# Layer 1 of a four-layer kernel begins on x and C alone, with TensorE on zeros until they come

## The chip, the cores and the metric

The kernel runs on one core of a Trainium2 chip. The metric is the device time of one execution in microseconds, lower is better. Before the change the median of three runs is 1193.91 us (1193.26 to 1196.67).

## The reference, cut to what matters

Four layers follow one another on x of 2048 x 576 (fp32): Fourier mixing, H3 convolution, Fourier mixing, H3 convolution. Each adds its result to x.

```python
def _A_ref(x, dft_seq_re, dft_seq_im, dft_hid_re, dft_hid_im):
    a = jnp.einsum("bsd,ed->bse", x, dft_hid_re)
    b = jnp.einsum("bsd,ed->bse", x, dft_hid_im)
    return jnp.einsum("ts,bse->bte", dft_seq_re, a) - jnp.einsum("ts,bse->bte", dft_seq_im, b)
...
x = x + _A_ref(_layernorm(x, axis=-1), ...)        # layer 1
x = x + _B_ref(_layernorm(x, axis=-1), B_k, B_v, B_shift_k, B_ssm_k, B_ssm_D)
x = x + _A_ref(_layernorm(x, axis=-1), ...)
x = x + _B_ref(_layernorm(x, axis=-1), B_k, B_v, B_shift_k, B_ssm_k, B_ssm_D)
```

`_B_ref` shifts k by a causal convolution of 4 taps, multiplies it with v, convolves that over the sequence with `ssm_k` by FFT, adds `ssm_D` times it, and multiplies with the normalised x. The FFT part doesn't depend on x, so one result serves both H3 layers.

## The kernel before, in words

**Layer 1** (`layer`, called with `get_x0`) multiplies the sequence DFT matrix C with the normalised x before the hidden DFT. Its work is cut into steps `(g, tb, k)`: for each of 4 blocks `tb` of 512 output columns, for the real and the imaginary matrix `g`, over 16 row blocks `k` of 128 rows. A step has 14 matmuls of 128x512: 12 into the four banks `s` (4 column groups of x, each high times high, high times low, low times high) and 2 into `rm`, which holds the remaining 64 columns. Every operand is split in a high part (rounded to fp32r by ScalarE) and a low part (the difference, by VectorE).

**A row of x** is loaded by SP (`load_x`), and gets its layer norm in pieces. `stats0` starts it: for rows 0 to 7 (`normed`, `norm_stats`) VectorE takes the statistics (lines 181 to 183) and GpSimd a power for the reciprocal root (line 184); then VectorE makes the bias (line 190) and ScalarE scales (line 191). From row `ASTAT` = 8 on (`normed_x`, `sums`) ScalarE sums (lines 649, 651), with GpSimd's power in line 653. `to_x` rounds (line 195) and makes the two low pieces (lines 197, 198). `get_x0(j)` does this for row j and starts the statistics of row j + 1; a step asks for the rows up to `XLEAD` = 3 ahead.

**A tile of C** is loaded by `load_c` into one of a few raw slots and split by `split` (lines 98 and 99) into one of three slots.

**The H3 stage** (`branch`, advanced by `next(br)`) fills VectorE, ScalarE and the gaps in TensorE's order meanwhile: it loads v, ssm_k, k and constants (`f1_loads`), splits rows (`f1_split`, lines 98 and 99), convolves k (lines 393 to 398), and multiplies with constants (`f1_products`, matmuls into the banks `bf`, which ScalarE evacuates in line 451). The main loop advances it to a wanted count at each half step, `want`, from `used` on. Six pieces are taken before the loop starts; with them come the first two H3 products, ahead of layer 1's first matmul.

**The order of the work** on each engine is a list scheduler's, which takes instructions by program order as they become ready in its own timing. `tc.issue_after(i)`, and `behind(...)` which nests several, queue what a block traces on the engine of `i` behind `i`; they order one engine's instructions and wait for no end. The lists `biased`, `rounded`, `made`, `halved`, `parted`, `stored`, `scaled` and `anchor` hold the instructions that serve as such marks: bias of a row, its rounding, its low half, the split of a C tile, that of an H3 row, an evacuation, a scaling, the load of a C tile. All loads of C, x and H3 rows share SP's queue; the H3 constants go through GpSimd's queue (`load_fr`), or through SP and a conversion on ScalarE when no power has been asked for yet.

Of the kernel before, what the change touches and what calls it, by code (L numbers as in the profile page):

```python
# [10 lines left out]
F32 = mybir.dt.float32  # L11
FR = mybir.dt.float32r
AF = mybir.ActivationFunctionType
OP = mybir.AluOpType

P = 128
# [3 lines left out]
J = S // P  # L20
TB = 4
NT = 512
# [3 lines left out]
EPS = 1e-5  # L26
ASTAT = 8
# [3 lines left out]
K_FIRST = 4  # L31
F1_16 = 5
VW = 384
F1_END = 42
W_FROM = 41
HOLD = 125
# [29 lines left out]
def fnet_h3_kernel(ctx: ExitStack, tc: tile.TileContext, x, c_mat, w_re, w_im, k_pad, v, shift_k,  # L66
                   ssm_k, ssm_d, f1c, i2c, midc, out):
    nc = tc.nc
# [5 lines left out]
    def mm(ps, lhsT, rhs, first, last, more=False):  # L74
        return nc.tensor.matmul(ps, lhsT, rhs, start=first, stop=last, skip_group_check=more).ins  # L75
# [3 lines left out]
    def turn():  # L79
        given[0] += 1  # L80
        return banks[(given[0] - 1) % 3]
# [15 lines left out]
    def split(h, l, src):  # L97
        a = nc.scalar.activation(h, src, AF.Copy).ins  # L98
        return a, nc.vector.tensor_tensor(l, src, h.bitcast(F32), OP.subtract).ins  # L99

    @contextmanager
    def behind(*instructions):
        with ExitStack() as stack:
            for i in instructions:
                stack.enter_context(tc.issue_after(i))
            yield
# [11 lines left out]
    def region_b(dt, name):  # L118
        return sb.tile([P, 6 * WIDE], dt, tag="rb", name=name)
# [9 lines left out]
    ring = {}  # L129

    def lay(t, at, *sizes):

        for name, words, n in sizes:
            ring.setdefault(name, Ring()).tiles.extend(t[:, at + i * words:at + (i + 1) * words] for i in range(n))
            at += n * words
        assert at <= t.shape[1], (at, t.shape, sizes)
        return at

    def fresh(*names):
        for name in names:  # L140
            ring[name] = Ring()
# [5 lines left out]
    xs = mats[:, :X_END].rearrange("p (j n) -> p j n", j=J)  # L147
# [13 lines left out]

    anchor, made, rounded, pows, biased, halved, added, evac, parted, stored = [], [], [], [], [], [], [], [], [], []

    scaled = []

    def load_after(dst, src):
        with tc.issue_after(anchor[-1]):
            return nc.sync.dma_start(dst, src).ins
# [8 lines left out]
    def norm_stats(src):  # L177
        m = ring["stat"]()
        st, mv, ve, rs = m[:, :12].rearrange("p (a c) -> p a c", a=2), m[:, 12:14], m[:, 14:15], m[:, 15:16]
        for i in range(2):  # L180
            nc.vector.bn_stats(st[:, i, :], src[:, i * HD:(i + 1) * HD])
        nc.vector.bn_aggr(mv, st)
        nc.vector.tensor_scalar(ve, mv[:, 1:2], EPS, None, op0=OP.add)  # L183
        pows.append(nc.gpsimd.tensor_tensor(rs, ve, mhalf, OP.pow).ins)  # L184
        return mv, rs, m[:, 16:17]

    def normed(src, y):
        mv, rs, nb = norm_stats(src)
        yield
        biased.append(nc.vector.tensor_scalar(nb, mv[:, 0:1], rs, -1.0, op0=OP.mult, op1=OP.mult).ins)  # L190
        scaled.append(nc.scalar.activation(y, src, AF.Identity, bias=nb, scale=rs).ins)

    def to_x(y, j):
        t = xs[:, j, :]
        rounded.append(nc.scalar.activation(t[:, :D], y, AF.Copy).ins)
        h = t.bitcast(F32)
        nc.vector.tensor_tensor(t[:, D:D + REM], y[:, NC * P:], h[:, NC * P:D], OP.subtract)
        made.append(nc.vector.tensor_tensor(t[:, D + REM:], y[:, :NC * P], h[:, :NC * P], OP.subtract).ins)
        return t
# [10 lines left out]
    X = [None] * J  # L210
    CT = {}

    def load_c(step):
        g, tb, k = step
        raw = ring["craw"]()
        anchor.append(load_after(raw, c_mat[g, tb, k]) if anchor else nc.sync.dma_start(raw, c_mat[g, tb, k]).ins)
        c = ring["cs"]()
        t = c[:, :NT], c[:, NT:]
        with behind(*stored):
            halved[:] = split(t[0], t[1], raw)  # L220
        CT[step] = t

# [77 lines left out]
    def layer(get_x, xres, done, pending, blocks=TB):  # L300
        steps = [(g, tb, k) for tb in range(blocks) for g in range(2) for k in range(J)]
        for n, (g, tb, k) in enumerate(steps):
# [3 lines left out]
            if n + 2 < len(steps):  # L306
                load_c(steps[n + 2])
# [41 lines left out]
    def branch():  # L349
# [3 lines left out]
        at = lay(flts, SC_AT + CRAW * NT, ("so", D, 4), ("land", D, 3))  # L353
        lay(flts, SC_AT + CRAW * NT, ("sp", 2 * VW, 3))
        lay(flts, at, ("craw", NT, 1))
# [103 lines left out]
        for n, (j, src) in enumerate(todo):  # L459
# [6 lines left out]
            elif src:  # L466
                visits += [(2 * n + 3, j, fcs[j], xf, at, VW, "sp", at) for at in range(0, 2 * D, VW)]
            if n:
# [203 lines left out]
    def normed_x(src, y, junk):  # L672
        sm, rs, nb = sums(src, junk)
        yield
        nc.vector.tensor_tensor(nb, sm, rs, OP.mult)
        nc.scalar.activation(y, src, AF.Identity, bias=nb, scale=rs)

    XL, LN = {}, {}

    def load_x(j):  # L680
        if j < J:
            XL[j] = ring["x"]()
            nc.sync.dma_start(XL[j], x[:, j, :])

    def stats0(j):
        if j < J and j not in LN:
            src = XL.pop(j)
            LN[j] = src, normed_x(src, src, ring["junk"]()) if j >= ASTAT else normed(src, src)
            next(LN[j][1])

    def get_x0(j):
        if X[j] is None:
            if j > 0:
                load_x(j + 2)
            stats0(j)
            if j > 0:
                with behind(*stored):
                    stats0(j + 1)
            src, ln = LN[j]
            with behind(*rounded[-1:]):  # L700
                next(ln, 0)
            X[j] = to_x(src, j)
# [32 lines left out]
    def done1(j, xa):  # L735
# [7 lines left out]
        if j < J - 1:  # L743
            nc.sync.dma_start(out[:, j, :], q)

    pending = []
    lay(flts, SC_AT, ("craw", NT, CRAW))
    br = branch()
    wl = load_w()
    load_x(0)  # L750
    next(br)
    get_x0(0)
    with tc.issue_after(biased[0]):
        next(br)
        with behind(*parted, scaled[0]):
            load_c((0, 0, 0))
        load_x(1)
        with behind(rounded[0]):
            load_c((0, 0, 1))
        load_x(2)  # L760
    used = 4
    first_lo = parted[1]
    next(br)
    next(br)
    with behind(first_lo):
        get_x0(1)
    next(br)
    next(br)
    spent = passed = 0.0
    total = (I2_END + 1 - MID_FROM) * STEP + 3 * 2 * TB * PIECE  # L770
    work = 64 * 3.1 + 32 * I2_COST
    for n, whole in layer(get_x0, lambda j: x[:, j, :], done0, pending):
        part = whole == "part"
        if part:
            whole = False
        if (whole or whole is not None and n % J < J - 1) and n <= F1_END and not part:
            at = n if whole else n - 0.5
            at16 = 4 + 2 * F1_16
            want = int(4 + F1_16 * at / 8 if at <= 16 else at16 + (68 - at16) * (at - 16) / (F1_END - 16))
            with behind(made[min(n + 2, J - 1)], *evac):  # L780
                while used < want:
                    next(br)
                    used += 1
        if whole is not None and not part and n >= W_FROM and len(W) < 9:
            with behind(*stored):
                next(wl)
        if whole and n == MID_LOAD:
            next(br)
        if n >= MID_FROM:
            if whole is not None:  # L790
                share = (5 if whole else 3) if n % J < J - 1 else (8 if whole else 6)
                passed += STEP * share / 14 * BORDER.get(n % J, 1.05)
            if whole is None or whole and n % 2 == 1 and n % (2 * J) < J - 1 and pending:
                finish(pending, 1)
                passed += PIECE
            while spent < work * min(1.0, passed / total):
                with behind(*added, *evac):
                    spent += next(br, work)
        if not whole:
            continue  # L800
        if n >= W_SAVE and n % 2 == 0:
            next(wl, 0)
        m = n - PREP
        if m == 0:
            lay(flts, SC_AT + CRAW * NT + 2 * D, ("xa", D, 2), ("yb", D, 2))
            old = ring["craw"]
            held = [old(), old()]
            fresh("craw")
            lay(flts, SC_AT + CRAW * NT + 6 * D, ("craw", NT, 1))
            ring["craw"].tiles.extend(held)  # L810
            gate = region_b(F32, "gate")
            lay(gate, 0, ("xa", D, 4), ("yb", D, 4), ("xj", D, 2))
        if 0 <= m and n < HOLD:
            advance(m // 2 if m % 2 == 0 and m < 2 * EARLY else None)
# [127 lines left out]
    cs, done = {}, []  # L942
# [67 lines left out]
    loaded, builds = [], []  # L1010
    for n, whole in layer(get_x1, lambda j: xb_d[j], done1, pending, 1):
# [12 lines left out]
        if n == STATIC:  # L1024
            t7.append(region_a(FR, "t7"))
            at = lay(flts, SC_AT + CRAW * NT, ("csum", WIDE, 3), ("rems", 2 * REM, 2))
# [27 lines left out]
    for ch in range(9):  # L1054
        first = ch + 2 if ch < 4 else ch + 6 if ch < 8 else 18
# [103 lines left out]
```

## Time and profile before

| | before |
|---|---|
| median of three runs | 1193.91 us |
| the profiled execution, its time | 1195.03 us |
| its span in the profile | 1193.3 us |
| TensorE busy | 1172.4 us, 98% of the span |
| VectorE busy | 840.3 us, 70% |
| ScalarE busy | 661.1 us, 55% |
| GpSimd busy | 75.6 us, 6% |
| mean granted TensorE clock | 0.998 |

A row of a timeline gives the start, the time that the piece took, the engine, the line and operation, what it writes from what it reads, its shape and number, and in brackets the idle time before it with what ended it. PE is TensorE, DVE VectorE, ACT ScalarE, POOL GpSimd; a q behind the name is the queue that issues DMAs. `s`, `rm` and `bf` are TensorE's banks, `mats` holds the split x and C, `flts` the fp32 work space, `early` the rows of x, `f1r` and `f1f` the H3 stage's tiles. A row of the waits names who waited, for whom, how long in all, how often and the longest.

### The profile page before, as it was taken

To read this page: it belongs to the slowest core of one execution; us is meant where nothing else is said; L and a number is where in the kernel's file an instruction comes from. 1 tells how busy PE (TensorE), PEld (TensorE's weight loads), DVE (VectorE), ACT (ScalarE), POOL (GpSimd) and SP (SyncE) were. 2 spreads that over 40 slices of the span, in tenths; PEclk is the share of its full clock that TensorE was granted. 3 is DMA by queue.
4 is the path that set the end of the run, shared out by engine and by line. 5 is a ranking of instruction groups with operands and counts; after the bars stand their busy time and mean duration, and the time that the engine had idled before them with its cause. 6 is when DMAs were issued, how large, how long until landed. Compare 5 with 4: busy or idle time off the path is not lost.

```text
span 1193.3 us, 18055 instructions
## 1 busy us (share of the span) xinstructions
PE 1172.4 (98%) x6248; PEld 996.3 (83%) x6248; DVE 840.3 (70%) x1498; ACT 661.1 (55%) x1311; POOL 75.6 (6%) x116
## 2 busy tenths in 40 slices
PE   7999999999999999999999999999999999999997
PEld 5776667888888888888988898888888888889997
DVE  7899983679777677685347756865776777774764
ACT  7865655679877668775435666634444445450210
POOL 2210000000000000001101121000000000001111
PEclk9999999999999999999999999999999999999999
DMA  9869898546666656648957676872672777895621
GB/s 327 306 199 311 263 295 269 167 133 188 217 194 211 206 174 203 207 133 272 295 193 236 230 246 226 267 260 71 220 277 76 220 278 258 248 334 158 217 86 41
DMA packets 142846, 259.85 MB, mean 218 GB/s; under 512 B 15649, under 2 KB 43553, under 8 KB 142754
## 3 DMA queue, kind: packets, MB, share of 16 engines
q1 hardware_dynamic: 102674, 205.45, 53.1%
q10 hardware_dynamic: 33168, 42.63, 10.3%
q0 software_dynamic: 6912, 10.62, 3.5%
q8 instruction: 49, 0.80, 0.3%
q14 instruction: 43, 0.35, 0.1%
HBM read 191.99 MB, written 66.65 MB: 217 GB/s over the span
## 4 chain that ended last, share of the span: by engine, by line
PE 76%; ACT 3%; DVE 1%; issue 1%; DMA 0%; POOLq 0%; ACTq 0%; DVEq 0%; SPq 0%
PE s L75 43%; PE bk L75 30%; PE rm L75 4%; ACT flts L512 1%; ACT mid L512 1%; ACT u L98 0%; DMA wd<-w 0%; ACT mats L98 0%; DVE mid L518 0%; DVE flts L534 0%; DVE flts L533 0%; DVE flts L531 0%; DVE flts L532 0%; DVE mats L99 0%; POOLq L1155 0%
## 5 line engine op out<-in xcount | busy, mean ns | idle before, releaser
L75 PE MATMUL s<-mats 128*128 128x512 f32 x2088 | 540.9, 395 | 2.4 <-DVE mats L99 0.8
L75 PEld LDWEIGHTS s<-mats 128*128 128x128 f32 x2088 | 380.9, 188 | 84.8 <-issue 10.4
L99 DVE TENSOR_TENSOR mats<-flts,mats 128x512 fp32r<-128x512 f32 x206 | 141.1, 689 | 63.8 <-ACT mats L98 62.5
L98 ACT ACTIVATE mats<-flts 128x512 fp32r<-128x512 f32 x206 | 128.5, 629 | 82.0 <-PE bk L75 35.0
L75 PE MATMUL bk<-mid 128*128 128x288 f32 x768 | 131.9, 298 | 2.4 <-ACT flts L512 1.6
L75 PEld LDWEIGHTS bk<-mid 128*128 128x128 f32 x768 | 116.9, 188 | 20.0 <-ACT flts L512 6.3
L75 PE MATMUL bk<-w,u 128*128 128x288 f32 x864 | 121.0, 296 | 0.4 <-DVE w L241 0.4
L75 PEld LDWEIGHTS bk<-w,u 128*128 128x128 f32 x864 | 117.5, 188 | 4.0 <-ACT flts L512 1.2
L518 DVE TENSOR_TENSOR mid<-flts,mid 128x576 fp32r<-128x576 f32 (+1 forms) x149 | 93.5, 628 | 34.9 <-ACT mid L512 30.9
L512 ACT ACTIVATE flts<-bk 128x288 f32<-128x288 f32 x160 | 62.1, 404 | 86.8 <-PE bk L75 77.7
L75 PE MATMUL rm<-mats 128*128 128x512 f32 x304 | 94.8, 391 | 0.0
L512 ACT ACTIVATE flts<-flts 64x288 f32<-64x288 f32 x192 | 85.0, 443 | 5.5
L512 ACT ACTIVATE mid<-flts 128x576 fp32r<-128x576 f32 (+1 forms) x148 | 80.4, 575 | 7.6 <-DMA flts<-td 3.2
L451 ACT ACTIVATE flts<-bf 128x384 f32<-128x384 f32 (+1 forms) x104 | 43.2, 463 | 45.6 <-PE bf L75 45.5
L287 DVE TENSOR_TENSOR flts<-flts,bk 128x288 f32<-128x288 f32 x48 | 21.8, 454 | 65.9 <-PE bk L75 65.8
L75 PE MATMUL bk<-mats 128*128 128x288 f32 (+1 forms) x376 | 67.8, 317 | 0.0
L75 PEld LDWEIGHTS rm<-mats 128*128 128x128 f32 x304 | 56.9, 188 | 12.3 <-DVE flts L273 0.2
L75 PE MATMUL s<-t,mats 128*128 128x512 f32 x264 | 64.9, 389 | 0.0
L184 POOL TENSOR_TENSOR flts<-flts 128x1 f32<-128x1 f32 x35 | 29.2, 834 | 522.0 <-DVE flts L183 520.0
L75 PE MATMUL bk<-mats,t 128*128 128x288 f32 (+1 forms) x368 | 59.3, 303 | 0.0
L75 PEld LDWEIGHTS bk<-mats 128*128 128x128 f32 x376 | 55.5, 188 | 3.4
L75 PEld LDWEIGHTS s<-t,mats 128*128 128x128 f32 x264 | 49.5, 188 | 10.3
(145 smaller groups left out, 1467.5 us busy)
## 6 DMA issues: line engine op xcount, KB each, us to landing
flts<-in_c_mat SPq DMA_DIRECT2D x148, 256.0 KB, 3.6
ph<-in_c_mat SPq DMA_DIRECT2D x54, 512.0 KB, 4.5
flts<-in_c_mat SPq DMA_DIRECT2D x30, 512.0 KB, 5.0
flts<-td SPq DMA_DIRECT2D x53, 288.0 KB, 3.0
td<-flts ACTq DMA_DIRECT2D x36, 384.0 KB, 4.5
vd<-flts ACTq DMA_DIRECT2D x64, 144.0 KB, 2.5
flts<-vd SPq DMA_DIRECT2D x32, 288.0 KB, 4.6
mid<-in_i2c POOLq DMA_DIRECT2D x32, 256.0 KB, 4.9
```

Source lines behind the costliest of these rows:

```text
L75: return nc.tensor.matmul(ps, lhsT, rhs, start=first, stop=last, skip_group_check=more).ins
L98: a = nc.scalar.activation(h, src, AF.Copy).ins
L99: return a, nc.vector.tensor_tensor(l, src, h.bitcast(F32), OP.subtract).ins
L184: pows.append(nc.gpsimd.tensor_tensor(rs, ve, mhalf, OP.pow).ins)
L287: added[:] = [nc.vector.tensor_tensor(r[:, cs], r[:, cs], ps[:, :HD], OP.add).ins]
L451: stored[:] = [nc.scalar.activation(so[:, i, :], ps[i], AF.Copy).ins]
L512: last_act.append(nc.scalar.activation(*args, **kw).ins)
L518: nc.vector.tensor_tensor(l, src, h.bitcast(F32), OP.subtract)
```

## The change

- SP's first loads become x row 0, C tile 0, x row 1, C tile 1, x row 2. The H3 stage's first loads follow behind row 2, and its first constant goes through GpSimd behind the power of row 1.
- `warm` clears 512 columns of the slot of row 15 on VectorE, and TensorE multiplies it with itself 18 times into a `bf` bank.
- The first C tile's high half is made ahead of row 0's scaling, its low half on VectorE behind the statistics of row 1. The rows 1 and 2 are started by hand, in a fixed order, ahead of the loop.
- Before the loop one piece of the H3 stage is taken instead of six; the wanted count is held to `2 * at - 2` in the first steps. The pieces queue behind later marks: the rounding of the row after, and up to step 7 the newest loads of x and C.
- In the loop, a row's statistics on VectorE queue behind the low half two rows before, for rows up to 7; the C split of the first 16 steps queues behind the rounding of row k - 2; x loads queue behind the newest C load. Rows from 8 on, whose statistics are ScalarE's, get no such mark.

```diff
+WARM = 18
...
-    scaled = []
+    scaled, varied = [], []
...
-        nc.vector.tensor_scalar(ve, mv[:, 1:2], EPS, None, op0=OP.add)
+        varied.append(nc.vector.tensor_scalar(ve, mv[:, 1:2], EPS, None, op0=OP.add).ins)
...
-    def load_c(step):
+    def raw_step(step):
         g, tb, k = step
         raw = ring["craw"]()
         anchor.append(load_after(raw, c_mat[g, tb, k]) if anchor else nc.sync.dma_start(raw, c_mat[g, tb, k]).ins)
+        return raw
+
+    def load_c(step, raw=None):
+        raw = raw_step(step) if raw is None else raw
         c = ring["cs"]()
         t = c[:, :NT], c[:, NT:]
-        with behind(*stored):
+        with behind(*stored, *rounded[step[2] - 2:max(0, step[2] - 1) if step[:2] == (0, 0) else 0]):
             halved[:] = split(t[0], t[1], raw)
...
-            nc.sync.dma_start(XL[j], x[:, j, :])
+            loaded.append(nc.sync.dma_start(XL[j], x[:, j, :]).ins)
...
             if j > 0:
-                load_x(j + 2)
+                with behind(anchor[-1]):
+                    load_x(j + 2)
             stats0(j)
             if j > 0:
-                with behind(*stored):
+                with behind(*stored, *made[j - 1:j if j < ASTAT - 1 else 0]):
                     stats0(j + 1)
...
+    def warm():
+        t = xs[:, J - 1, :NT]
+        nc.vector.memset(t.bitcast(F32), 0.0)
+        b = turn()
+        for i in range(WARM):
+            mm(b, t[:, :P], t, i == 0, i == WARM - 1)
...
     load_x(0)
-    next(br)
-    get_x0(0)
-    with tc.issue_after(biased[0]):
+    raws = []
+    for i in range(2):
+        with behind(loaded[-1]):
+            raws.append(raw_step((0, 0, i)))
+        with behind(anchor[-1]):
+            load_x(i + 1)
+    warm()
+    stats0(0)
+    first = ring["cs"]()
+    CT[0, 0, 0] = first[:, :NT], first[:, NT:]
+    nc.scalar.activation(first[:, :NT], raws[0], AF.Copy)
+    next(LN[0][1], 0)
+    with behind(biased[0]):
+        stats0(1)
+    with behind(loaded[-1]):
         next(br)
-        with behind(*parted, scaled[0]):
-            load_c((0, 0, 0))
-        load_x(1)
-        with behind(rounded[0]):
-            load_c((0, 0, 1))
-        load_x(2)
-    used = 4
-    first_lo = parted[1]
-    next(br)
-    next(br)
-    with behind(first_lo):
-        get_x0(1)
-    next(br)
-    next(br)
+    with behind(varied[1]):
+        low = nc.vector.tensor_tensor(first[:, NT:], raws[0], first[:, :NT].bitcast(F32), OP.subtract).ins
+        X[0] = to_x(LN[0][0], 0)
+    with behind(made[0]):
+        next(LN[1][1], 0)
+    with behind(biased[1], rounded[0]):
+        load_c((0, 0, 1), raws[1])
+    with behind(halved[1]):
+        stats0(2)
+    used = -1
...
-            want = int(4 + F1_16 * at / 8 if at <= 16 else at16 + (68 - at16) * (at - 16) / (F1_END - 16))
-            with behind(made[min(n + 2, J - 1)], *evac):
+            want = int(min(2 * at - 2, 4 + F1_16 * at / 8) if at <= 16 else at16 + (68 - at16) * (at - 16) / (F1_END - 16))
+            with behind(made[min(n + 2, J - 1)], *evac, *rounded[min(n, 4) + 1:min(n, 4) + 2],
+                        *(loaded[-1:] + anchor[-1:] if n < 8 else [])):
```

More of the change, by code (lines that the diff above doesn't have):

```diff
@@ L676, in normed_x @@
         nc.scalar.activation(y, src, AF.Identity, bias=nb, scale=rs)
[L678 removed]
+    XL, LN, loaded = {}, {}, []
     def load_x(j):
```

## The prediction

> **What bounds the kernel now.** I read the page first, then the waits of TensorE, then the timelines of TensorE and of all engines over the first 60 us, since the diff touches nothing that runs later than layer 1's first blocks.
>
> ```profile
> span 1193.3 us, 18055 instructions
> PE 1172.4 (98%) x6248; PEld 996.3 (83%) x6248; DVE 840.3 (70%) x1498; ACT 661.1 (55%) x1311; POOL 75.6 (6%) x116
> ```
>
> TensorE is busy for 1172.4 of 1193.3 us, so 20.9 us is all the idle time there is. The waits say where much of it lies:
>
> ```profile
> PE bf L75 <- DVE f1r L99: 6.7, 1, 6.7
> PE bf L75 <- ACT flts L451: 1.2, 2, 1.1
> PE s L75 <- DVE mats L99: 0.8, 1, 0.8
> PE s L75 <- ACT mats L195: 0.8, 1, 0.8
> ```
>
> The first 6.7 us are the wait for the first operand; the fourth line is one stall inside block 0 (at 55.6 us, below). What this leaves out is how fast TensorE runs once it has started. Its timeline:
>
> ```profile
> 6.71 1.09 PE L75 MATMUL bf<-f1r 64*128 64x288 f32 x6 [6.71 <-DVE f1r L99]
> 7.94 0.79 PE L75 MATMUL s<-mats 128*128 128x512 f32 x1
> 9.58 0.79 PE L75 MATMUL s<-mats 128*128 128x512 f32 x1 [0.84 <-DVE mats L99]
> 10.40 1.09 PE L75 MATMUL bf<-f1r 64*128 64x288 f32 x6
> 11.42 3.86 PE L75 MATMUL s<-mats 128*128 128x512 f32 x10
> 15.12 0.62 PE L75 MATMUL rm<-mats 128*128 128x512 f32 x2
> 15.57 2.90 PE L75 MATMUL s<-mats 128*128 128x512 f32 x12
> 18.31 0.62 PE L75 MATMUL rm<-mats 128*128 128x512 f32 x2
> 18.77 2.88 PE L75 MATMUL s<-mats 128*128 128x512 f32 x12
> 22.03 0.67 PE L75 MATMUL bf<-f1r 64*128 64x288 f32 x6
> 22.63 3.05 PE L75 MATMUL s<-mats 128*128 128x512 f32 x12
> 27.42 0.66 PE L75 MATMUL bf<-f1r 64*128 64x288 f32 x6
> 29.95 2.88 PE L75 MATMUL s<-mats 128*128 128x512 f32 x12
> ```
>
> Twelve matmuls of 128x512 run from 15.57 to 18.31, 0.228 us each; the ten from 11.42 to 15.12 took 0.370 each. An H3 product (six bf matmuls) is 1.09 us twice at the beginning and 0.66 later. So TensorE runs slow until it has been dense for some time. If a slow matmul takes twice a fast one (the products bound the ratio below, at 1.65), 6.2 of the ten were slow, and the fast rate came at 11.42 + 6.2 x 0.456 = 14.25, that is 3.85 us after the dense run began at 10.40.
>
> From 15.57 on TensorE has no gap up to 55 us. A step (12 s and 2 rm matmuls) is 18.77 - 15.57 = 3.20. A product adds 22.63 - 22.03 = 0.60, or up to 0.78 with its gaps when it stands inside a step; I take 0.70. By 29.95 five steps and four products are done: 5 x 3.20 + 4 x 0.70 = 18.8 us of work. **Lost up to there: 29.95 - 18.8 = 11.15 us.** This is the quantity the change works on.
>
> **The change part by part.** The chain that brings the first matmul of layer 1, and the loads beside it, now:
>
> ```profile
> 0.74 0.39 SPq L683 DMA_DIRECT2D early<-in_x  x1
> 0.81 0.06 DVE L174 MEMSET flts<- 128x1 f32 x1 [0.81 <-PEq L1151]
> 1.18 0.42 SPq L418 DMA_DIRECT2D flts<-in_ssm_k  x1
> 3.76 0.82 DVE L181 BATCH_NORM_STATS2 flts<-early 128x6 f32<-128x288 f32 x2 [2.89 <-DMA early<-in_x]
> 4.48 0.68 ACT L98 ACTIVATE f1r<-flts 128x576 fp32r<-128x576 f32 x1 [2.24 <-DMA flts<-in_ssm_k]
> 4.62 0.21 DVE L182 BATCH_NORM_AGGREGATE flts<-flts 128x2 f32<-128x12 f32 x1
> 4.86 0.15 DVE L183 TENSOR_SCALAR flts<-flts 128x1 f32<-128x1 f32 x1
> 5.10 0.55 POOL L184 TENSOR_TENSOR flts<-flts 128x1 f32<-128x1 f32 x1 [4.65 <-DVE flts L183]
> 5.68 0.21 DVE L190 TENSOR_SCALAR flts<-flts 128x1 f32<-128x1 f32 x1 [0.67 <-POOL flts L184]
> 5.93 0.87 ACT L191 ACTIVATE early<-early,flts 128x576 f32<-128x576 f32 x1
> 7.23 0.67 ACT L195 ACTIVATE mats<-early 128x576 fp32r<-128x576 f32 x1
> 7.75 1.18 DVE L181 BATCH_NORM_STATS2 flts<-early 128x6 f32<-128x288 f32 x3 [1.19 <-DMA early<-in_x]
> 8.85 0.68 DVE L99 TENSOR_TENSOR mats<-flts,mats 128x512 fp32r<-128x512 f32 x1
> 9.44 0.22 DVE L197 TENSOR_TENSOR mats<-early,mats 128x64 fp32r<-128x64 f32 x1
> 9.57 0.68 DVE L198 TENSOR_TENSOR mats<-early,mats 128x512 fp32r<-128x512 f32 x1
> ```
>
> *x and C alone.* x row 0 stays the first load, so its statistics still begin at 3.76 and its bias still ends at 5.89. The C tile moves to the second place on SP; what is second today (288 KB) landed at 4.48, so C's high half (0.61 on ScalarE) is made by 5.1, ahead of the scaling. The scaling stays at 5.93. Rounding no longer stands behind a C split: 5.93 + 0.89 + 0.67 = 7.5 instead of 7.90. The first operand pair is ready at 7.5.
>
> *The low halves.* Row 1 of x, in the fifth place today, was waited for until 7.75; in the third it has 832 KB up to its end (288 + 256 + 288) against 1248 (288 + 288 + 128 + 256 + 288). Between row 0 at 3.7 and 7.75, in proportion to the bytes, that is 6.05 (bounds 5.5 and 6.6). The new order sends VectorE through row 1's statistics before C's low half: 6.05 + 0.86 + 0.24 + 0.1, so C low at 7.25 to 7.92 and x low, by the spacings of 8.85, 9.44 and 9.57, at 7.97 to 8.65. Today they end at 9.53 and 10.25. A low-half product that must wait until 8.7 delays a column by at most 8.7 - 7.5 - 0.46 = 0.75; high products of the other three columns, 0.9 us and more of them, can stand in between if the scheduler puts them there. Cost between 0 and 0.75; I take 0.1, since the high halves are ready sooner in any timing.
>
> *Row 1 in time for step 1.* GpSimd's power for row 1 falls among VectorE's three two-input operations. Rows that show what this does:
>
> ```profile
> 11.27 0.73 DVE L429 TENSOR_TENSOR flts<-flts,f1f 1x576 f32<-1x576 f32 x1
> 11.45 0.99 POOL L184 TENSOR_TENSOR flts<-flts 128x1 f32<-128x1 f32 x1 [5.16 <-DVE flts L183]
> 49.10 2.62 DVE L393 TENSOR_TENSOR f1f<-f1f 128x1152 f32<-128x1152 f32 x2
> 49.27 4.13 POOL L653 TENSOR_TENSOR flts<-flts 128x1 f32<-128x1 f32 x1 [7.69 <-DVE flts L652]
> ```
>
> A power is 0.55 alone, 0.99 when it was issued inside a two-input operation of VectorE (it ended 0.44 after it), and 4.13 when such operations followed one another. So row 1's ends at 8.65 + 0.44 = 9.1, its bias at 9.3, scaling and rounding at 10.9, its low half near 11.75. Step 0, dense from 7.6, ends at 10.8: a wait of 0.1 to 0.3, I take 0.2. Rows 2 and 3 follow at 2.4 to 2.8 us each by the same spacings, below the 3.20 of a step, so the lead grows.
>
> The Trainium skill (SBUF — State Buffer, "Who interferes with whom") says that a VectorE instruction with two SBUF inputs contends with a GpSimd instruction that reads SBUF, and the later one blocks fully; the two pairs of rows above agree (0.99 and 4.13 against 0.55). By it the change, which puts such operations beside row 1's power, could lose what it wins; what that gives here is the case of the held powers, below.
>
> *Zeros.* A memset of 128x512 on VectorE is not in the trace; it lies between the 0.06 of the 128x1 memset and the 0.68 of a two-input 128x512 operation, ends between 0.9 and 1.6, and hides under the wait for x until 3.76. TensorE begins near 1.5. Slow for 3.85 us, that is 8.4 matmuls at 0.456; the other 9.6 at 0.228 take 2.2: the zeros end at 7.55, just when x is ready. If the slow time is 4.9 (10.40 to 15.3, the latest the rows allow) they end at 8.05; all slow, at 9.7. They cost between 0 and 0.55 (2.2 if they never bring the fast rate, the third case) and I take 0.05.
>
> The Trainium skill (TensorE: Matmul & The Clock Gate, Part 1) says that the array runs at half clock until a free-running window of about 3.4 us has been busy. The 3.85 above fits; by this rule the zeros would end between 7.2 and 8.8, and the sum would come out the same or up to 1.2 us later.
>
> *The H3 stage.* Its first loads move behind x row 2 on SP, its constants to the GpSimd queue behind row 1's power, its two first products from before step 0 into step 3. By the wanted counts both versions have taken eight pieces by the end of step 4 (before 6 + 2, after 1 + 7), so the same four products are done there, at the fast rate. Two products in each of steps 3 and 4 ask ScalarE for about 0.7 + 0.7 more a step than now; the lead of the rows pays for it, as this rounding of row 8 shows, done while TensorE is still at row 5 (the step that begins at 29.95):
>
> ```profile
> 31.81 0.69 ACT L195 ACTIVATE mats<-early 128x576 fp32r<-128x576 f32 x1
> ```
>
> New SP orders (x and H3 loads behind the newest C load) put loads behind C loads that wait for a raw slot; that slot is free one step before. I take 0 for both; if a lead is gone the price is the third case.
>
> **Sum.** Lost after the change: 7.5 (first operands) + 0.05 (zeros) + 0.1 (low halves) + 0.2 (row 1) = 7.85. Gain 11.15 - 7.85 = **3.3 us**, bounds 2.1 (0.75, 0.55 and 0.3 all paid) and 3.65 (all dense from 7.5). Behind step 4 the order of work is as before and TensorE-bound, so the shift holds to the end. The profiled execution: span 1193.3 becomes 1190.0, with 1.7 us around it (1195.0) 1191.7; the median of the runs, 1193.9, stands 1.1 under the profiled run, so 1190.6.
>
> **The rivals.**
>
> *Block 0's stall goes too.*
>
> ```profile
> 55.65 0.67 ACT L195 ACTIVATE mats<-early 128x576 fp32r<-128x576 f32 x1
> ```
>
> TensorE waited 0.8 us for this rounding of row 12, whose power is the one that took 4.13. In another phase of VectorE's convolution the power takes 0.55 and the stall vanishes: gain 3.3 + 0.8 = 4.1, 1189.8. For it: the early pieces are reshuffled. Against it: behind step 4 the same orders stand.
>
> *The start is eaten.* Either the zeros don't bring the fast rate (9.7 at the end of the zeros, then 3.85 us at half rate cost another 1.9: lost 11.6, 1194.4), or row 12, which has no slack, doesn't come 3.3 us sooner, because its chain hangs on VectorE and GpSimd and not on TensorE, and the stall grows to 4.1: 1193.9. Against the second: ScalarE waits on TensorE too (its evacuations and ring slots), so its pace follows.
>
> *Slower: held powers.* Rows 9 to 15 get their powers from GpSimd while VectorE runs the convolution's two-input operations. Each power held as at 49.27 delays its row by 4.13 - 0.55 = 3.6. It decides as soon as the row's slack is under 3.6, which 3.3 us less lead brings about. Two more held rows: 2 x 3.6 - 3.3 = 3.9 slower, 1197.8. Against it: one such row in seven now.
>
> *It doesn't do what it says:* matmuls on zeros queued late or x not first would show a first real matmul near 7.9 and no gain; it is part of the third case.
>
> **How the numbers follow.** Forecast 0.50, stall gone 0.26, eaten 0.10, slower 0.14. A measurement of this kernel tells about 0.3%, 3.6 us, from no change; the forecast's own range, 1189.6 to 1191.8 (its bounds, and the 0.65 by which the fastest run shown lies under the median), has four tenths of its chance beyond that bound. Faster 0.26 + 0.20 = 0.46, same 0.30 + 0.10 = 0.40, slower 0.14. The range leaves out the slower case and takes in the rest: from 1188.8 (3.65 and 0.8 gained, 0.65 of scatter) to 1194.6 (eaten, with 0.7).
>
> **What would show it.** Right: zeros from about 1.5 to 7.6; first s matmul on x between 7.5 and 8; ten s matmuls of step 0 at 0.228; the fifth step ending near 26.7 instead of 29.95; TensorE's busy time up by the zeros, about 6 us. Wrong in a step: row 0's statistics later than 3.8 (loads), s matmuls at 0.37 after 8 (zeros don't count), a wait on mats L195 or L198 in steps 1 to 4 (rows late), a wait on flts L451 in steps 3 and 4 (evacuations). Wrong altogether: a fifth step at 27 and the end not earlier, which would put the loss into rows 9 to 15 or behind them.

## The result: 0.9% slower, and the profile after

After the change the median of five runs is 1207.05 us (1204.66 to 1207.64), beside 1194.33 for the kernel before in the same session: ratio 1.0091, 95% interval 1.0072 to 1.0111 (the ratios here and below are not quotients of the medians shown). The forecast was 1190.6, its range ended at 1194.6. The profiled execution took 1207.05, its span is 1205.3, 12.0 more than before.

The page of the kernel after, then its waits of TensorE:

```profile
span 1205.3 us, 18096 instructions
PE 1180.1 (98%) x6266; PEld 1000.5 (83%) x6266; DVE 840.7 (70%) x1499; ACT 659.8 (55%) x1310; POOL 76.8 (6%) x117
```

```profile
PE bf L76 <- DMA f1r<-in_f1c: 6.0, 1, 6.0
PE bk L76 <- ACT flts L517: 4.0, 10, 1.3
PE bk L76 <- DVE flts L292: 1.5, 2, 0.8
PE bf L76 <- DVE mats L754: 1.5, 1, 1.5
```

TensorE's share is 98% as before: it is busy 7.7 us longer, of which the 18 zeros are 6.5. The wait of 6.7 us for the first operand became one of 1.5 (for the memset of the zeros). Two others are new or larger: one of 6.0 us appeared, on a DMA that brings an H3 constant, and `bk`, the accumulators of layer 2's stage, far from the diff, waited 1.6 and 0.7 us for evacuations before and 4.0 and 1.5 after. The timeline of TensorE shows the start and the wait for the constant:

```profile
1.49 6.70 PE L76 MATMUL bf<-mats 128*128 128x512 f32 x18 [1.49 <-DVE mats L754]
8.03 3.24 PE L76 MATMUL s<-mats 128*128 128x512 f32 x12
11.57 2.88 PE L76 MATMUL s<-mats 128*128 128x512 f32 x12
22.72 3.02 PE L76 MATMUL s<-mats 128*128 128x512 f32 x12
32.24 1.09 PE L76 MATMUL bf<-f1r 64*128 64x288 f32 x6 [6.05 <-DMA f1r<-in_f1c]
33.26 4.83 PE L76 MATMUL s<-mats 128*128 128x512 f32 x12
37.93 0.61 PE L76 MATMUL rm<-mats 128*128 128x512 f32 x2
```

Up to 26.2 us it looks as forecast, with steps 0 to 4 dense and from step 1 on at the fast rate, but two H3 products are done by then and not the four forecast. Then nothing for 6.05 us, and the work behind it is slow again: a product of 1.09 and a step's 12 matmuls in 4.67 (33.26 to 37.93) instead of 2.74. The windows of the same stretch, whose columns are the stretch, its length, the busy time and number of instructions of each engine, the granted clock of TensorE, the DMA share and GB/s:

```profile
26.20:32.20 6.00, 0.00 (x0) 0.00 (x0) 2.62 (x6) 2.42 (x6) 0.70 (x2) 0.85 1.07 372
32.24:33.26 1.02, 1.02 (x7) 0.74 (x7) 0.00 (x0) 0.00 (x0) 0.00 (x0) 0.50 1.13 382
33.26:37.23 3.97, 3.97 (x11) 3.13 (x10) 1.99 (x5) 3.62 (x8) 0.56 (x1) 0.51 0.90 348
37.23:41.00 3.77, 3.77 (x21) 2.79 (x19) 1.83 (x4) 1.80 (x5) 0.00 (x0) 1.00 0.09 35
```

The clock falls in the wait (0.85 as a mean), stays at 0.5 for the next 5.0 us and is full from 37.2 on. So the constant costs 6.05 + 0.43 (product) + 1.93 (step) = 8.4 us. Why it was late stands in GpSimd's timeline and in the DMA view of 20 to 34 us:

```profile
8.72 0.69 POOL L173 DMA_DIRECT2D f1r<-in_f1c  x1
23.53 0.55 POOL L185 TENSOR_TENSOR flts<-flts 128x1 f32<-128x1 f32 x1 [3.32 <-DVE flts L184]
24.03 0.58 POOL L173 DMA_DIRECT2D f1r<-in_f1c  x1
```

```profile
f1f<-in_k_pad SPq DMA_DIRECT2D x3, 576.0 KB, 8.7
f1f<-in_shift_k SPq DMA_DIRECT2D x2, 576.0 KB, 9.8
f1r<-in_f1c POOLq DMA_DIRECT2D x3, 128.0 KB, 8.3
```

One constant serves two products. The first is asked for behind row 1's power, at 8.72. The second, which the third product needs at 26.2, is asked for only behind row 6's power, at 24.03, and takes some 8 us to land, among 2.9 MB that SP has just asked for. Before, it was asked for behind row 0's power, far ahead of the third product, which ran at 22.03:

```profile
5.10 0.55 POOL L184 TENSOR_TENSOR flts<-flts 128x1 f32<-128x1 f32 x1 [4.65 <-DVE flts L183]
5.60 0.69 POOL L172 DMA_DIRECT2D f1r<-in_f1c  x1
```

The table follows the kernels all the way. It gives how much later (or, with a minus, earlier) the same `s` or `rm` matmul, counted from layer 1's first, starts than before, in us; the header gives the place by the clock of before. At 26 us the kernels with the change have done one H3 product (0.6 us) less than before; from 56 us on the numbers agree.

| profile | 26 (step 4) | 56 (step 12) | 127 | 256 | 536 | end |
|---|---|---|---|---|---|---|
| after | -3.2 | +7.6 | +8.3 | +8.7 | +12.5 | +12.3 |
| before again (e5) | +0.1 | +0.1 | -0.2 | -0.2 | -0.2 | -0.1 |
| before, banks fixed (e9) | +0.9 | +1.0 | +0.9 | +1.3 | +1.2 | +1.6 |
| four constants early (e2) | -3.8 | +0.2 | +0.3 | +0.8 | +4.7 | +6.0 |
| tiny zeros (e6) | -0.1 | -0.1 | -0.9 | -0.7 | +2.3 | +3.0 |
| tiny zeros, banks fixed (e10) | +0.8 | +0.8 | +0.4 | +1.7 | +1.7 | +2.2 |
| after, banks fixed (e11) | -2.6 | +7.2 | +7.2 | +7.4 | +8.8 | +9.0 |
| zeros, banks fixed (e13) | -1.1 | -2.0 | -2.6 | -2.1 | -1.7 | -1.6 |

After: -2.6 at step 4 with the one missing product counted (-3.2 + 0.6), +8.4 for the constant, about +2.5 from there to 127 us, +4 from 127 us to the end, where the diff changes nothing. Three theories came out of this: the late constant (A), rows of x that cannot follow a faster TensorE (B), and something that changes layer 2's stage (C).

### The profile page after: what moved, and what is told of

Same layout as the page of the kernel before. It is cut to its first block, busy times and chain, and to the rows that moved or that the text cites. A ratio compares the mean times of both kernels' runs of the same rounds, so it can differ in the third digit from the quotient of the medians.

```text
span 1205.3 us, 18096 instructions
## 1 busy us (share of the span) xinstructions
PE 1180.1 (98%) x6266; PEld 1000.5 (83%) x6266; DVE 840.7 (70%) x1499; ACT 659.8 (55%) x1310; POOL 76.8 (6%) x117
## 4 chain that ended last, share of the span: by engine, by line
PE 72%; ACT 4%; DVE 3%; DMA 2%; issue 1%; ACTq 0%; POOL 0%; DVEq 0%; SPq 0%; POOLq 0%
PE s L76 40%; PE bk L76 28%; PE rm L76 4%; ACT flts L517 2%; ACT mid L517 1%; DMA flts<-td 1%; DVE mid L523 1%; DMA flts<-in_c_mat 0%; ACT mats L99 0%; ACT u L99 0%; DVE u L100 0%; DMA wd<-w 0%; DVE flts L538 0%; DVE mats L100 0%; DVE flts L537 0%
```

## The experiments

**The constant (A).** In e1 the second constant is asked for behind row 1's power as the first is, and the later ones behind the latest power as in the kernel after. In e2 the first four are asked for behind row 1's power.

```diff
     def load_fr(dst, src):
-        with tc.issue_after(pows[-1]):
+        with tc.issue_after(pows[min(1, len(pows) - 1)] if len(pows) < ASTAT else pows[-1]):   # e1
+        with tc.issue_after(pows[1] if 1 < len(pows) < 12 else pows[-1]):                      # e2
```

> The changed kernel, with the constant of H3 row 0 queued on GpSimd behind row 1's power and not behind row 6's; those of rows 2 and 3 stay behind row 7's (one edit). Theory, late constant: TensorE's wait of 6.05 us for it goes, and with it the second slow stretch (0.4 + 1.9); the next constant, asked for at 25.3 as now, may be late in its turn by up to 4 us. So 1207.05 - 8.4 = 1198.6, up to 1202.6 if the wait moves to the next constant. Rival, bunched loads (SP sends some 2.9 MB of k, shift and x rows at 20.2 to 22.5): whatever is asked for, something waits about as long, 1205 to 1208. Rival, the products in steps 3 and 4 are too early for the split rows: the same product waits for ScalarE or VectorE, over 1203.

> The changed kernel, with the constants of the first four H3 rows all queued behind row 1's power. Late constant: no wait on f1r in TensorE's order at all, the fifth step done near 26.7, and at most 1198.6; the start's gain of 2.5 us comes through and only later stalls keep it above the kernel before. Bunched loads: the four constants of 128 KB go out beside x and C at 10 us and delay those, a new wait on mats in steps 2 to 4, over 1203.

Measured: e1 1200.32 us, ratio 1.0038 (1.0026 to 1.0051); e2 1200.75, 1.0038 (1.0024 to 1.0052). The wait on the DMA is gone in both. In e2 the constants go out together and the third product runs at 26.21:

```profile
8.05 2.29 POOL L173 DMA_DIRECT2D f1r<-in_f1c  x4
```

```profile
26.21 0.67 PE L76 MATMUL bf<-f1r 64*128 64x288 f32 x6 [0.54 <-DVE f1r L100]
48.09 2.11 PE L76 MATMUL s<-mats 128*128 128x512 f32 x8 [0.67 <-DVE mats L100]
53.49 2.12 PE L76 MATMUL s<-mats 128*128 128x512 f32 x8 [0.70 <-DVE mats L100]
56.55 1.91 PE L76 MATMUL s<-mats 128*128 128x512 f32 x6 [0.72 <-ACT mats L196]
```

A is shown: asking for one constant earlier is worth 0.53% (1.0091 to 1.0038), 6.3 us of the 8.4 counted above; both runs stayed some 2 us above the 1198.6 expected. And both are still slower than before, though e2 is ahead by 3.8 us at step 4 (3.2 with the missing product counted). Its lead is gone by step 12, in part at the three waits of 48 to 57 us (2.1 us), where before has only the last (0.8). Behind 127 us it loses another 5.7; that is the question of C.

**The zeros.** e3 is the kernel after without `warm`; e4 is the kernel before with 14 zeros right behind the load of row 0.

```diff
     load_x(0)
+    warm()          # e4, WARM = 14; e3 instead takes this line out of the kernel after
```

> The changed kernel without the memset and the 18 matmuls on zeros. Late constant: TensorE starts near 7.4 but slow, about 1.3 us behind at step 4, and meets the same constant at the same time, so the wait shrinks by that much and the end stays within 1 us of 1207. If zeros cost something by themselves (clock, power, the late start at 8.03), it is faster by 1 or more; if they were worth their full price it would be slower by 1.3.

> The kernel before with one part of the change alone: the memset and 14 matmuls on zeros (until about 6.7) ahead of the first product. If the zeros bring the fast rate, the first two products, the first two s matmuls and the ten after them run fast: 0.43 + 0.4 + 0.43 + 1.43, of which what stands ahead of a wait for data is hidden; gain 1.5 to 2.7, 1191.6 to 1192.8. If zeros don't count, the time stays at 1194.3.

Measured: e3 1206.49, 1.0088 (1.0075 to 1.0102): in the kernel after, the zeros bring nothing that lasts. Without them TensorE is slow at first and 1.6 us further behind at step 4, and the wait for the same constant is 1.1 us shorter for it:

```profile
PE bf L76 <- DMA f1r<-in_f1c: 4.9, 1, 4.9
```

e4: 1196.68, 1.0006 (0.9997 to 1.0014), where a gain of 1.5 to 2.7 us or none was expected. Its profiled execution is at the upper end of its runs; counted as in the table, it is 3.0 us ahead at 127 us and 2.8 behind at the end. The loss lies far behind the zeros.

**What moves layer 2's stage (C).** e5 is the kernel before once more. e6 has 14 zero matmuls of 8 columns, which warm nothing (its first product takes 1.09 us, as in before).

```diff
-            mm(b, t[:, :P], t, i == 0, i == WARM - 1)          # e4
+            mm(b[:, :8], t[:, :P], t[:, :8], i == 0, i == WARM - 1)   # e6
```

> The kernel before, unchanged, for a second profile of it. The kernel with zeros alone is 3.0 us ahead at the start of layer 2 (near 210 us) and 2.8 behind at the end, and the one with four constants goes from 0.3 to 6.0 behind in the same stretch, though every engine's order is the same from 150 us on. If that is a matter of the profiled execution (the runs of before spread from 1193.3 to 1197.6), this profile differs from the first by 2 us or more between 210 and 1050 us. If it belongs to the kernels, the two profiles of before agree within 1 us there.

> The kernel before with the 14 matmuls on zeros 8 columns wide: as many instructions on TensorE as in the kernel with zeros alone, but over in about a us, so that TensorE starts slow as before. If the instructions' number alone moves the later part (fetches fall elsewhere), 2 to 3 us slower than before, 1197.5. If the later loss comes from starting earlier, the same as before, 1195.6.

Measured: e5 1195.21, 0.9993 (0.9984 to 1.0002); e6 1198.09, 1.0018 (1.0009 to 1.0027). From step 1 on the two executions of before agree to 0.4 us, but for 0.7 near 215 us, so the loss behind 256 us is not scatter; and e6 shows that it needs no shift of TensorE at the start. The order of the instructions on each engine is the same in all these kernels from about 160 us on, but for one pair of SP's loads near 686 us in the kernels with the change. What differs is the bank that a `bk` accumulator gets: `bank()` draws from a pool of three, and the scheduler gives out the one that is free in its own timing. With the three banks named in the order of their first use, 194 of 294 accumulators in e6 have another bank than before, in the kernel after 211, from the sixth on. A matmul that needs the bank that was evacuated last has to wait for the evacuation. Such a wait in e6 (before has none at this place):

```profile
458.39 0.66 PE L76 MATMUL bk<-mid 128*128 128x288 f32 x3 [0.69 <-ACT flts L513]
```

**The banks held.** Four kernels take before's sequence of banks, written out, in place of the pool: before itself (e9, the control), e6 (e10), the kernel after (e11) and e7 (e12, below). The zeros take the third bank of the H3 products' rotation and not its next one, so that the products keep before's banks too.

```diff
+BANKS = "21021021021210201202102012021020..."     # 244 banks, those of the kernel before
...
     def bank():
-        return psp.tile([P, NT], F32, tag="b", bufs=3, name="bk")
+        n = next(picked, None)
+        return psp.tile([P, NT], F32, tag="b", bufs=3, name="bk") if n is None else banks[int(n)]
...
-        b = turn()
+        b = banks[2]          # in warm: e10, e11, e12
```

> Control: the kernel before, with the PSUM bank of each of the first 244 bk accumulators written out as the scheduler had chosen it there, instead of taken from whichever is free. Every engine's order is the same but for 24 matmuls near 560 us. 1195.6, no change; what differs is the cost of writing it out.

> The kernel with 14 tiny zeros (1198.1), with the bank sequence of the kernel before written out. From the sixth bk accumulator on the scheduler had given other banks than before, though each engine's order was the same. Theory, banks: the 2.5 us go, 1195.6. Rival, fetches or the number of instructions: 1198.1 again.

> The changed kernel with the bank sequence of the kernel before written out. Theory, banks: what it loses between 215 and 540 us (4 us against the kernel before) goes, 1202.5 to 1204; the late constant and the rows stay. Rival, a late start carries on into layer 2 by loads and evacuations: 1206 to 1207.

Measured: e9 1195.51, 1.0003 (0.9994 to 1.0012); e10 1196.54, 1.0007 (0.9998 to 1.0016); e11 1204.06, 1.0072 (1.0058 to 1.0085). Writing the banks out costs nothing in time (e9). The profiled execution of e9 is 0.9 us behind before from the first step on, where the two have the same order of work and TensorE stayed slow for longer, so e10's row of the table is best read against e9's. The waits of e6, e10 and e11 for these evacuations (the banks are all named `bf` in the last two, and the line numbers shift):

```profile
PE bk L76 <- ACT flts L513: 2.9, 10, 0.7
PE bk L76 <- DVE flts L288: 1.5, 2, 0.8
```

```profile
PE bf L81 <- ACT flts L521: 1.5, 6, 0.4
PE bf L81 <- DVE flts L296: 0.7, 1, 0.7
```

```profile
PE bf L81 <- DMA f1r<-in_f1c: 5.4, 1, 5.4
PE bf L81 <- ACT flts L525: 2.5, 8, 0.9
PE bf L81 <- DVE flts L300: 1.6, 2, 0.8
```

With before's banks the tiny zeros have before's waits (1.5 and 0.7) and lose no more between 256 and 536 us (table), with as many instructions as e6. What e10 loses between 127 and 256 us is one wait of 1.3 near 213 us, where e5, which is before itself, has one of 0.9. The kernel after gains 0.19%, some 2.3 us, and drifts 1.8 from 127 us to the end instead of 3.9. In both pairs the intervals of the two ratios overlap, so there the profiles carry the argument.

They say it place by place. At 335 and at 530 us (by the clock of before) TensorE waits 0.24 to 0.32 us in each of the eight kernels with another sequence of banks (after, e1 to e4, e6 to e8), and at 457 us, the place of the row shown above, 0.2 to 1.0 us in five of them. Before has no wait at the three places, nor has any of the eight kernels with its banks held (e9 to e16). So these waits belong to the banks; in the kernel after they are 1.2 us. Two larger ones do not belong to them: near 274 us the kernel after waits 1.3 and e11 still 0.9, and near 433 us 0.7 and 0.8, as here in e13 (below), which has before's banks:

```profile
431.92 1.06 PE L81 MATMUL bf<-mid 128*128 128x288 f32 x6 [0.83 <-DVE flts L296]
```

C is shown for the first three places. What makes the waits at 274 and 433 us stays open; the one at 274 us occurs only in kernels with the changed start.

**The rows (B).** e7 is e2 with the statistics of rows 8 and 9 on VectorE instead of ScalarE; e8 is e2 without the new marks on VectorE's rows; e12 is e7 with the banks held.

```diff
-ASTAT = 8
+ASTAT = 10                                                     # e7, e12
...
-                with behind(*stored, *made[j - 1:j if j < ASTAT - 1 else 0]):
+                with behind(*stored, *made[:0]):               # e8
```

> The kernel with four constants asked for early, and the statistics of rows 8 and 9 on VectorE and GpSimd's first form (ASTAT 10), which takes about 3.6 us off ScalarE. Theory, ScalarE's backlog: ScalarE is idle for 3.1 of the 10 us from 10 to 20 us, against 1.3 before, and busy for over 9 of 10 between 20 and 60, so the rows don't come sooner and TensorE waits for them in steps 10 to 12 (2.1 us in three gaps); with less work on ScalarE those gaps go, gain 1.5 to 2.5 against the kernel with four constants (1200.8). Rival, VectorE and GpSimd pace the rows: VectorE gets 2 us more, the powers are held longer, the gaps stay or grow, 1200.5 to 1203.

> The kernel with four constants asked for early, without the mark that queues a row's statistics on VectorE behind the low half two rows before (the loop's only; the order by hand for rows 1 and 2 stays). If the mark holds the early rows back and leaves ScalarE idle from 10 to 20 us, rows 3 to 7 come sooner, ScalarE's idle time there goes back towards 1.3 and the gaps of steps 10 to 12 shrink, 1198.5 to 1200. If the chain of row and power sets the pace, no change, 1200.8; if the mark protects the low halves from statistics that are not yet due, TensorE waits on mats L100 or L199 in steps 1 to 4, 1202.

> The changed kernel with the four constants asked for early, rows 8 and 9 on VectorE, and the bank sequence of the kernel before. If the late constant, ScalarE's backlog and the banks are the whole loss, what is left is the start's gain less what the rows still cost: 1198.0 less 3 to 4 for the banks, 1194 to 1195.5, the same as the kernel before or up to 1.5 us faster. If the banks are not a cause, 1198.

Measured: e7 1198.03, 1.0013 (1.0004 to 1.0022); e8 1204.59, 1.0069 (1.0056 to 1.0081); e12 1196.73, 1.0012 (1.0003 to 1.0021). Two rows off ScalarE are worth 2.7 us (e7 against e2), so ScalarE was late in e2. Holding the banks brought e12 no gain over e7 that the ratios show, where 3 to 4 us were expected: its waits at 274 and 433 us, 1.4 and 0.5, are among those that stay with before's banks. Without the marks the low half of the first C tile comes late, and later a row; the timeline of TensorE in e8:

```profile
10.90 3.46 PE L76 MATMUL s<-mats 128*128 128x512 f32 x9 [2.19 <-DVE mats L781]
55.54 1.54 PE L76 MATMUL s<-mats 128*128 128x512 f32 x4 [2.09 <-ACT mats L196]
```

So the marks are what keeps step 0 dense. With all three mended (e12) the kernel is still not faster than before: 2.5 us ahead at step 4 (1.9 with the missing product counted), 0.6 behind at step 12. That left two questions, tried in two pairs.

**More relief for the rows?** e15 is e12 with rows 10 and 11 on VectorE too; e16 is e12 with fewer H3 pieces asked for in the first 16 steps.

```diff
-ASTAT = 10
+ASTAT = 12        # e15
-F1_16 = 5
+F1_16 = 4         # e16
```

> e12 with the statistics of rows 10 and 11 on VectorE too (ASTAT = 12). If ScalarE's backlog in steps 4 to 12 eats the start's gain: TensorE's waits between 48 and 57 us shrink from about 1 us to under 0.4, and the time is 0.5 to 1.5 us under e12 (about 1195.5, ratio 1.0000 to 1.0008). If VectorE is as full there as ScalarE, or its two-input operations hold the powers: the same as e12 or up to 2 us more, with waits on rows made by VectorE.

> e12 with 12 instead of 14 H3 pieces wanted by step 16 (F1_16 = 4), the rest later. If the H3 pieces on ScalarE and VectorE are what makes rows 9 to 13 late: TensorE's waits between 48 and 57 us go, and the time is 0.5 to 1.5 us under e12. If the work only moves behind step 16, where it is as tight: the same as e12, or up to 2 us more with new waits after 60 us.

Measured: e15 1198.42, 1.0027 (1.0013 to 1.0041); e16 1199.5, 1.0040 (1.0028 to 1.0053). Both expectations of a gain failed. Each moves the wait to the other engine or to a later place; one row of the timeline of TensorE in each:

```profile
54.44 2.12 PE L81 MATMUL s<-mats 128*128 128x512 f32 x8 [2.02 <-DVE mats L108]
```

```profile
72.48 3.00 PE L81 MATMUL s<-mats 128*128 128x512 f32 x12 [2.38 <-DVE u L108]
```

In e15 VectorE makes a C tile's low half late, in e16 the loss comes at the end of block 0, where VectorE evacuates `u` behind the H3 work that was put off. More relief for ScalarE alone does not help, then. That VectorE and ScalarE together set the pace is the reading that fits, though no run shows it: each is busy for about 80% of the time. The sums of the windows over the first 60 us, for before and for e2:

```profile
sum 60.00, PE 51.50 PEld 38.67 DVE 47.93 ACT 49.89 POOL 15.35; mean PE 8.58 PEld 6.45 DVE 7.99 ACT 8.31 POOL 2.56
```

```profile
sum 60.00, PE 55.56 PEld 40.70 DVE 48.09 ACT 48.64 POOL 16.98; mean PE 9.26 PEld 6.78 DVE 8.01 ACT 8.11 POOL 2.83
```

By 60 us the two have done no more in e2 (96.7 us of work) than in before (97.8), though TensorE had been ahead. ScalarE's share is lost between 10 and 20 us, where the windows of before and of e2 have it busy for 8.73 and 6.94:

```profile
10.00:20.00 10.00, 9.97 (x39) 7.71 (x39) 9.58 (x34) 8.73 (x17) 4.55 (x7) 1.00 1.07 377
```

```profile
10.00:20.00 10.00, 10.00 (x47) 7.62 (x46) 8.55 (x29) 6.94 (x12) 3.24 (x5) 1.00 1.03 328
```

The H3 work that was put off there is asked for again where the rows need both engines. That an order exists which keeps the lead is neither shown nor excluded.

**Zeros in front of the old order.** e13 is e4 with the banks held, e14 the same with 12 zeros, which end before the first operand is ready.

```diff
-WARM = 14
+WARM = 12        # e14
```

> The kernel before with 14 matmuls on zeros at the start and before's choice of banks written out. If the banks are what ate the zeros' gain: 2 to 3 us under before (about 1193, ratio 0.9975 to 0.9985), with the lead of 3 us at 210 us still there at the end. If the lead is lost by itself wherever TensorE next waits for an evacuation: about 1196, as e4 (ratio 1.0006).

> As e13 with 12 zeros, which end at about 6.7 us, when the first operand is ready (14 ended at 7.55). If each 0.1 us at the start counts to the end: 0.3 to 0.8 us under e13. If the clock needs the 14 (the first products at 1.09 again): the same or up to 1 us above e13.

Measured: e13 1194.20 us, beside 1195.36 for before on the same chip: 0.9987 (0.9978 to 0.9995); e14 1193.80, 0.9986 (0.9977 to 0.9994). Both are faster than before, by 0.13%, 1.2 to 1.6 us, where 2 to 3 were expected of e13; the two can't be told apart. Against e4 (1.0006, 0.9997 to 1.0014) the intervals don't meet, so the banks decide whether the zeros gain: from 127 us to the end e4 loses 5.8 us and e13 1.1. The start of e14's timeline:

```profile
1.49 4.81 PE L81 MATMUL bf<-mats 128*128 128x512 f32 x12 [1.49 <-DVE mats L757]
6.77 0.67 PE L81 MATMUL bf<-f1r 64*128 64x288 f32 x6 [0.47 <-DVE f1r L108]
14.51 3.04 PE L81 MATMUL s<-mats 128*128 128x512 f32 x12 [1.14 <-ACT mats L204]
```

The first product, 1.09 us in before, takes 0.67. Row 1 isn't ready for the faster TensorE (a wait of 1.14), which leaves a lead of 0.9 at step 4. Row 12's stall of 0.8 at 56 us is gone, and the lead is 1.8 there.

## Why the prediction was wrong, step by step

Of the start, the timeline of the kernel after:

```profile
4.20 0.63 ACT L774 ACTIVATE mats<-flts 128x512 fp32r<-128x512 f32 x1 [1.96 <-DMA flts<-in_c_mat]
5.73 0.87 ACT L192 ACTIVATE early<-early,flts 128x576 f32<-128x576 f32 x1 [0.90 <-DVE flts L191]
6.63 0.69 ACT L196 ACTIVATE mats<-early 128x576 fp32r<-128x576 f32 x1
7.81 0.96 POOL L185 TENSOR_TENSOR flts<-flts 128x1 f32<-128x1 f32 x1 [2.36 <-DVE flts L184]
```

*x and C alone: right.* C's high half was made by 4.83 (forecast: by 5.1), the scaling began at 5.73 (5.93), the rounding of row 0 ended at 7.32 (7.5).

*The low halves and row 1: right.* Step 0's 12 `s` matmuls took 3.24 us and step 1's 2.88, so 0.36 was lost to the low halves (0.1 taken, 0.75 the bound). Row 1's power took 0.96, about as the held one of before (0.99), and step 1 had no wait (0.2 taken). That the lead of the rows then grows was too much, though: in e11 and e12, which start the same way, step 2 waited 0.80 and 0.89 for row 2. The rule of the Trainium skill that was weighed (SBUF — State Buffer, "Who interferes with whom") agrees with this 0.96 and cost no more than that.

*Zeros: right in kind; their size is another in each execution.* The memset took 0.48. The zeros ended at 8.03, 0.7 behind the rounding; 0.05 was taken and 0.55 the bound. The windows of the zeros, up to the matmul in which the rate changes and behind it:

```profile
1.49:6.35 4.86, 4.86 (x11) 1.00 0.88 264
6.35:8.02 1.67, 1.67 (x8) 1.00 1.03 389
```

and the same slow part in e13 and in e14:

```profile
1.49:6.78 5.29, 5.29 (x13) 1.00 0.97 294
```

```profile
1.49:5.44 3.95, 3.95 (x10) 1.00 0.91 276
```

Eleven in 4.86 us, then seven and the first `s` matmul in 1.67: the slow stretch was 4.9 us, not the 3.85 worked out from a mean of step 0. It was 5.3 in e13, 4.0 in e14 and 5.0 behind the wait. Over the twelve kernels that begin with zeros of full width it runs from 3.2 (e2, e12) to 5.7 (e4); in e2 the zeros were done by 7.4, about as forecast (7.55). The clock column reads 1.00 in all four windows, also where a matmul took 0.43 us; at the start of an execution the slow rate shows in the matmuls alone. It also ends at another time in each execution: the ten matmuls of step 0, 3.86 us in the trace of before that the forecast rests on, took 4.11 in e5 and 4.63 in e9, with the same order of work:

```profile
11.44 4.63 PE L80 MATMUL s<-mats 128*128 128x512 f32 x10
```

So the 11.15 us lost that the forecast starts from are one execution's, and e9's are 0.9 more. The Trainium skill (TensorE: Matmul & The Clock Gate, Part 1) has a busy window of about 3.4 us for the full clock, a window that runs free of the kernel. The runs agree with about one window as the least (3.2) and show that it is not the time to expect (up to 5.7). All in all the start gained 2.6 us where 3.3 was forecast.

*The H3 stage: the step that failed.* "New SP orders ... I take 0 for both", and its premise one part earlier: "its constants to the GpSimd queue behind row 1's power". `load_fr` queues behind `pows[-1]`, the latest power traced so far. Only the constant that is traced before the loop meets row 1's; taking one piece instead of six before the loop moved the next behind row 6's. The prediction counted the pieces that are done by step 4 and not where each of their loads is issued. The late constant cost 8.4 us, 6.05 of waiting and 2.4 of a slow clock, against 0; asking for it earlier gave 6.3 of that back (e1). The count itself was off too: at the end of step 4 two of the four products forecast were done, and in e2, without the wait, three.

*"The lead of the rows pays for it": wrong as well.* With the constant early (e2) the lead of 3.8 us at step 4 is gone at step 12. The second half of the third rival, that rows hang on VectorE and GpSimd and not on TensorE, comes nearest: two rows' statistics moved off ScalarE gave 2.7 us (e7), so the rows did not follow TensorE, and the ground for refusal, "ScalarE waits on TensorE too", did not hold in steps 4 to 12. It was named for row 12 alone and it was a matter of several, and ScalarE was part of what held them.

*"Behind step 4 the order of work is as before and TensorE-bound, so the shift holds to the end": wrong by about 4 us (behind 127 us).* The order was the same and the banks were not, and the waits for evacuations changed: 1.2 us of them in the kernel after belong to the banks, 2.1 (at 274 and 433 us) came without a cause that a run shows.

*The rivals.* The slower case had the right sign and the wrong cause: held powers took up to 3.60 in e2, against 4.13 in before, and are no part of the account. That block 0's stall would go was seen, but in e4, e13 and e14. Of the signs listed, "a fifth step at 27 and the end not earlier" comes near to what happened: five steps were done at 26.2, with two products fewer than forecast.

## What to carry to other kernels

When a change delays a stage, follow each load that the stage issues to the mark it queues behind at the moment it is traced; a mark written "behind the latest one" moves with everything that is moved past it. An early start is worth what the engines that feed it can follow, so sum the feeding engines' work up to the first place without slack before counting the shift to the end. And where a pool's buffers are given out in the scheduler's own timing, hold the sequence before comparing variants: here the banks were worth 0.19% (e4 against e13), and the whole gain that was forecast is 0.3%.

## What the runs showed of the hardware beyond expectation

- A wait of 6.05 us cost TensorE 2.4 us more at a granted clock of 0.5. Waits of a third of that went either way: behind 2.19 and 2.09 us in e8 the matmuls took 0.384 and 0.385 us each, at a granted clock of 0.63; behind 2.38 in e16 they took 0.250.
- From a cold start TensorE ran slow for 3.2 us (e2) to 5.7 (e4), with the zeros begun at 1.49 us in both; and before itself took 3.86, 4.11 or 4.63 us for the same ten matmuls (before, e5, e9).
- Twelve zero matmuls are enough to make the first product fast (0.67 for 1.09), across a gap of 0.47.
- A 128 KB constant took 5.8 us to land as a median in the first 60 us of before and 8.3 among large loads in the kernel after.
- With the order of work nearly the same, another choice among three PSUM banks moved the time by 0.19% (e4 against e13).
